# Decay factors carried into the transposing matmuls of q, x copied by ScalarE, and unit 2's norm placed one unit earlier

## The chip, the cores and the metric

The kernel runs on one core of a Trainium2 chip. The engines of that core work side by side, each through its own queue of instructions in order: TensorE (in the profile PE for matmuls, PEld for weight loads), VectorE (DVE), ScalarE (ACT), GpSimd (POOL) and SyncE (SP), which only issues transfers here. A matmul writes to PSUM, of which the kernel has eight banks. The metric is the device time of one execution in microseconds (us); the times given are of several executions, and their median is compared.

## The reference

Two blocks are computed one after the other. The first is a retention layer: attention without softmax, whose scores are weighted by a power of a decay factor for each head.

```python
batch, n_heads, seq, head_dim = (8, 8, 576, 64)
scores = scale * np.matmul(q, k.transpose(0, 1, 3, 2))          # scale = 1/sqrt(64)
gamma = 1.0 - 2.0 ** (-5.0 - np.arange(H))                      # one per head
Dmat = np.where(rel >= 0, gamma[:, None, None] ** rel, 0.0)     # rel = row - column
ret = scores * Dmat
attn_out = np.matmul(ret, v)
```

Its output, with the heads side by side, is x: 8 * 576 = 4608 tokens of 512 numbers. The second block is a feed-forward layer with RMS norm:

```python
rms = np.sqrt(np.mean(x * x, axis=-1, keepdims=True) + 1e-06)
xn = x / rms * rms_g
g = xn @ w_gate                                                 # 512 x 1536
out = (g * (1.0 / (1.0 + np.exp(-g))) * (xn @ w_val)) @ w_out   # 1536 x 512
```

q, k, v and the norm's weights are 32-bit floats; the three large weight matrices come as 64-bit floats and are turned to 32 bits in the kernel.

## The kernel before

**Retention.** There are 32 jobs, one for each batch and pair of heads (`jobs`, line 127). A sequence of 576 is cut into nine chunks of 64 (`L`). Within a chunk the scores are multiplied by v directly (`values`); what earlier chunks contribute is carried in a running sum of k times v (`states` and `sums`) and multiplied by q (`carried`). The decay is split into factors: k's part is put on v by ScalarE (`scale_v`, table `gv`), a constant power of gamma and the causal mask on the scores (`weigh`, line 312), a factor for a whole chunk on the running sum (`gc`), and q's part, gamma to the power of the position in the chunk plus 64, over 8, on the result: `carried` multiplies the two PSUM banks `av` by the table `gq` on VectorE as it writes x (lines 389 to 394). Jobs from 8 on put odd chunks in swapped halves of a bank (`column`) and so also need `gx`, the same table with its halves swapped.

q and k are needed with head elements on the partitions. From job 8 on VectorE transposes them (`prepare`). For the first eight jobs TensorE does it (`turn`, line 216): four 128-token blocks of q for each of two heads as matmuls with the identity `ident` as the moving operand, four blocks of k as transposes, then the last 64 tokens of each as one transpose; ScalarE copies the banks to `qT` and `kT` (lines 235 and 244).

One `slot(j)` (line 397) issues `values` of job j-1, `scores` and `states` of job j, VectorE's `weigh` and `sums` of job j, and `carried` of job j-1. Between `values` and `carried` stands a memset of `tick` on POOL (line 359), which waits for the last matmul of `values`; the first matmul of `carried` waits for it. All these share five PSUM banks (`banks`); three more hold `s`, the scores and states.

**Feed-forward.** x is taken in twelve units of 384 tokens (`U`). Units 0 and 1 go through plain matmuls into the hidden layer (`up_plain`); units from 2 on through a scheme of seven half-size block products instead of eight (`up`). The product with `w_out` uses seven block products for all units (`across`, a generator that hands over after each product). The sums of weight blocks that the scheme needs are made by `combine(m)` on POOL (line 803), twelve 128x512 operations for each of the two weight matrices, and by `combine_out` on VectorE for `w_out`. The hidden layer of unit 1 lies in the part of `w_up[1]` that `combine(1)` writes; the part of `w_up[0]` that `combine(0)` writes holds sums that `across` of units 0 and 1 reads.

**Norm of a unit.** `norm_0`: four squares on ScalarE and three adds on VectorE. `norm_1`: three matmuls with a column of 1/512 into a bank `ms`, an add on VectorE, a power on POOL. `diagonals`: three diagonal matrices on VectorE. `norm_2`: a matmul `rb`, four products that scale x, and, from unit 2 on, four subtractions for the block scheme.

**Order.** The schedule is written out by hand: every engine's queue has its work in program order. `start()` (line 846) loads the tables and the first eight jobs, runs slots 0 to 7 with the turns of the next job between them and with steps of the weights' conversion spread among them (`weights`, `act`), then `up_plain` of units 0 and 1, `across(1)` and `across(0)`. Around these last two stand `combine(1)`, slot 8, unit 2's norm, `combine(0)` and slot 9. Loads are issued by SP, some by ScalarE. The tile framework gives the transfers of both queues eight semaphores in turn, so that one waits for the landing of the one eight before it. From unit 2 on a loop runs `up` and `across` with the other slots between.

Of the kernel before, what the change touches and what calls it, by code (L numbers as in the profile page):

```python
# [10 lines left out]
F32 = mybir.dt.float32  # L11
# [3 lines left out]
P = 128  # L15
# [7 lines left out]
def _decay_tables(H, D):  # L23

    pairs = _gamma(H).reshape(H // 2, 2).T
    rows = np.repeat(pairs, D, axis=0)
    pos = np.arange(L)
    p = np.concatenate([pos, pos])  # L30
    gq = rows[:, :, None] ** (pos + L) / np.sqrt(D)
    t = pairs.T[None] ** -p[:, None, None], rows**L, gq, np.roll(gq, D, axis=0)
    return [np.ascontiguousarray(x).astype(np.float32) for x in t]


# [6 lines left out]
def kernel(  # L42
# [64 lines left out]
    gx = const.tile([P, NHP, L], F32, name="gx")  # L107
    gv = const.tile([P, NHP, 2], F32, name="gv")
    gc = const.tile([P, NHP], F32, name="gc")
    tick = const.tile([1, 1], F32, name="tick")  # L110
    rms_g = const.tile([P, NHP], F32, name="rms_g")
    w_out = const.tile([P, NF, DM], F32, name="w_out")
# [87 lines left out]
    def load_kv(j):  # L200
# [12 lines left out]
            out=t, in_=v[b, 2 * hp : 2 * hp + 2, NFULL * P :].rearrange("e p d -> p e d")  # L213
        )

    def turn(j):

        d = st[j]
        last = bank(f"turn_{j}_t")
        for nm in "qk":  # L220
            ps = bank(f"turn_{j}_{nm}")
            for c in range(NFULL):
                if nm == "k":
                    nc.tensor.transpose(
                        out=ps[:, c * P : c * P + P],
                        in_=d["k"][:, c].rearrange("p e d -> p (e d)"), identity=ident,
                    )
                    continue
                for e in range(2):
                    nc.tensor.matmul(  # L230
                        ps[side(e), c::NFULL], lhsT=d["q"][:, e, c], rhs=ident,
                        start=True, stop=True,
                    )
            t = d[nm + "T"] = att.tile([P, S], F32, tag=nm + "T", name=f"{nm}T_{j}")
            nc.scalar.copy(out=t[:, : NFULL * P], in_=ps)
        for i, nm in enumerate("qk"):
            o = slice(i * TAIL, i * TAIL + TAIL)
            nc.tensor.transpose(
                out=last[:, o], in_=d[nm + "t"].rearrange("p e d -> p (e d)"),
                identity=ident[:TAIL, :TAIL],  # L240
            )
        for i, nm in enumerate("qk"):
            o = slice(i * TAIL, i * TAIL + TAIL)
            nc.scalar.copy(out=d[nm + "T"][:, NFULL * P :], in_=last[:, o])
# [117 lines left out]
    def carried(j):  # L362

        d = st[j]
        b, hp = jobs[j]
        av = d["av"]
        for c in range(1, NC):
            i, odd = divmod(c, 2)
            for e in range(2):
                mm = nc.tensor.matmul(  # L370
                    av[odd][column(j, odd, e), i * L : i * L + L], lhsT=d["sum"][side(e), c - 1],
                    rhs=d["qT"][side(e), c * L : c * L + L],
                    start=False, stop=(c >= NC - 2), skip_group_check=True,
                )
                if c == 1 and e == 0:
                    follow(mm, d["valued"])
        for c0, c1 in ((0, 2 * HU), (2 * HU, S)) if b % 2 == 0 else ((0, HU), (HU, S)):
            u, o = divmod(b * S + c0, U)
            if u not in x_of:
                x_of[u] = xp.tile([P, NHP, U], F32, tag="x", name=f"x_{u}")  # L380
            x = x_of[u][:, hp, o : o + c1 - c0].rearrange("p (c k) -> p c k", k=L)
            for first in (c0 // L, c0 // L + 1):
                i, odd = divmod(first, 2)
                n = -(-(c1 // L - first) // 2)
                moves = [(slice(0, P),) * 2]
                if column(j, odd, 0) != side(0):
                    moves = [(side(e), column(j, odd, e)) for e in range(2)]
                for to, at in moves:
                    g = (gq if to == at else gx)[at, hp].unsqueeze(1)
                    nc.vector.tensor_tensor(  # L390
                        out=x[to, first - c0 // L :: 2],
                        in0=av[odd][at, i * L : (i + n) * L].rearrange("p (c k) -> p c k", k=L),
                        in1=g.to_broadcast([at.stop - at.start, n, L]), op=ALU.mult,
                    )
        st[j] = {}
# [450 lines left out]
    def start():  # L846

        h_of[0] = ffn.tile([P, NF, U], F32, tag="h", name="h_0")
        tables = list(zip((causal, gv, gc, gq, gx), (_causal_table(), *_decay_tables(H, D))))

        def table(i, queue):
            t, values_ = tables[i]
            src = nc.inline_tensor(values_, name=t.tensor.name + "_table")
            queue.dma_start(out=t, in_=src.ap())

        make_identity(nc, ident)
        nc.scalar.activation(out=tick, in_=mhalf[:1], func=AF.Silu)
        nc.vector.memset(ones, 1.0)
        warm = bank("warm")
        for _ in range(6):  # L860
            nc.tensor.matmul(warm[:, :P], lhsT=ones, rhs=ones, start=True, stop=True)
        first_places.update(find_places())
        load_chunks(1)
        for i in (1, 0, 2):
            table(i, nc.scalar)
        weights(3)
        for j in range(2 * NHP):
            load_first(j, {0: range(2), 1: range(2, H), NHP: range(H)}.get(j))
            if j == 1:
                table(3, nc.sync)  # L870
            load_chunks((1, 1, 1, 1, 2, 2, 2, 3)[j], nc.sync)
        table(4, nc.sync)
        nc.sync.dma_start(out=rms_g, in_=moe_rms_g.rearrange("(c p) -> p c", p=P))
        load_chunks(4, nc.sync)
        turn(0)
        scale_v(0)
        act(3)
        squares = []
        for j in range(2 * NHP):
            slot(j)  # L880
            if j + 1 < 2 * NHP:
                turn(j + 1)
            if squares:
                gather(*squares.pop())
            for i in ((1,), (2,), (3,), (4, 5), (6,), (7,), (), ())[j]:
                scale_v(i)
            if j:
                u, c = divmod(j - 1, NHP)
                squares.append((u, c, square(u, c)))
            act(1)  # L890
            if j == 5:
                norm_1(0)
            elif j == 6:
                norm_2(0)
            weights((2, 0, 0, 1, 1, 1, 1, 0)[j])
            if j == 4:
                gather(*squares.pop())
            elif j == 5:
                diagonals(0)
            act(1)  # L900
        gather(*squares.pop())
        load_qk(2 * NHP)
        load_kv(2 * NHP)
        made = combine_out()
        for m, g in [(m, g) for g in range(NG) for m in range(2)]:
            for u in range(2):
                weights_to(4 * g + 2 * m + 1)
                for i, _ in enumerate(up_plain(u, m, g)):
                    if not (u or m or g):
                        if i == 0:  # L910
                            values(2 * NHP - 1)
                            carried(2 * NHP - 1)
                            gather(1, NHP - 1, square(1, NHP - 1))
                        elif i == 1:
                            norm_1(1)
                        elif i == 2:
                            diagonals(1)
                        elif i == 3:
                            norm_2(1)
                    weights(2)  # L920
                    act(1)
                    if u and m and g == NG - 1:
                        weights_to(len(chunks))
                        next(made, None)
                    if i == 1:
                        weights_to(4 * g + 2 * m + 2)
        for _ in made:
            pass
        for blk, t in first_blocks.items():
            keep(blk, t)  # L930
        rest = across(1)
        next(rest)
        following(2 * NHP - 1)
        for _ in rest:
            pass
        rest = across(0)
        next(rest)
        combine(1)
        slot(8, rest=False)
        following(8)  # L940
        for i, _ in enumerate(rest):
            if i in (1, 2, 4):
                (norm_0, norm_1, norm_2)[i // 2](2)
                if i == 2:
                    diagonals(2)
        combine(0)
        slot(9)
        following(9)
# [71 lines left out]
```

## Time and profile before

| | |
|---|---|
| median of 5 executions | 1154.46 us (1152.39 to 1158.57) |
| profiled execution | 1158.57 us, span 1156.8 us, mean granted clock of TensorE 0.993 |
| TensorE busy | 1130.3 us, 98% of the span, 10524 matmuls |
| VectorE busy | 719.2 us (62%) |
| ScalarE busy | 244.0 us (21%) |
| POOL busy | 51.2 us (4%) |
| DMA | 125.42 MB, 108 GB/s on average |
| first matmul of `up_plain` | at 61.6 us |
| `across(1)`, `across(0)` | 191.4 to 218.9 us, 220.0 to 253.5 us |
| first matmul of `up` for unit 2 | at 256.4 us |

All times are counted from the start of the span. In a line of a timeline stand the start, the duration, the engine, the line of the kernel, the operation, what is written and read, the shape and the count; in square brackets the time that the engine stood idle before it and what ended that. In a list of waits stand the one who waited and what it waited for, then the total, the number of times and the longest. "issue" means that the engine waited for nothing that the profile shows. A 32-bit matmul shows as two instructions.

### The profile page before, as it was taken

How to read it: one execution, taken by the hardware profiler on the slowest of the kernel's cores; microseconds unless marked ns; L12 is line 12 of the kernel's file. 1: busy time of each engine (PE TensorE's matmuls, PEld its weight loads, DVE VectorE, ACT ScalarE, POOL GpSimd, SP SyncE). 2: the span in 40 equal slices, each digit the busy share in tenths (PEclk: the TensorE clock that was granted, in tenths of full speed). 3: DMA queues.
4: the chain of work that ended last, by engine and by line, in shares of the span. 5: the costliest groups of instructions: out<-in, count | busy, mean ns of one | idle time of the engine just before them, and what ended most of it. 6: DMA issues, size and time to landing. Idle time of an engine off the chain costs nothing.

```text
span 1156.8 us, 24803 instructions
## 1 busy us (share of the span) xinstructions
PE 1130.3 (98%) x10524; PEld 1056.5 (91%) x10524; DVE 719.2 (62%) x1420; ACT 244.0 (21%) x480; POOL 51.2 (4%) x74
## 2 busy tenths in 40 slices
PE   8899999988999999999999999999999999999998
PEld 7655557988999999999999999999999999999998
DVE  5698867576576575465775776465576576445352
ACT  5545641101211221111220220120220210120210
POOL 0000000480000000000000000000000000000000
PEclk9899999999999999999999999999999999999999
DMA  8765336324553646025335456306436403403304
GB/s 204 202 164 168 109 108 207 64 50 107 132 121 49 167 128 139 39 89 116 96 95 95 106 129 140 116 17 128 104 95 137 130 34 92 128 1 97 122 1 110
DMA packets 292943, 125.42 MB, mean 108 GB/s; under 512 B 270432, under 2 KB 275808, under 8 KB 292832
## 3 DMA queue, kind: packets, MB, share of 16 engines
q1 hardware_dynamic: 282688, 107.66, 37.8%
q10 hardware_dynamic: 10144, 16.16, 4.3%
q8 instruction: 83, 1.36, 0.5%
q14 instruction: 28, 0.23, 0.1%
HBM read 108.83 MB, written 14.94 MB: 107 GB/s over the span
## 4 chain that ended last, share of the span: by engine, by line
PE 87%; DVE 6%; DMA 2%; issue 1%; ACT 1%; SPq 1%; DVEq 0%; POOL 0%; ACTq 0%; POOLq 0%
PE w L507 13%; PE x L507 13%; PE z L507 13%; PE up L564 8%; PE xo L629 7%; PE wo L629 7%; PE zo L629 7%; PE y L507 7%; PE yo L629 4%; PE av L351 2%; PE av L370 2%; PE s L280 1%; PE s L300 1%; DMA w_gate<-in_moe_w_out_dram 1%; DVE sum L329 1%
## 5 line engine op out<-in xcount | busy, mean ns | idle before, releaser
L531 ACT COPY m<-x 128x384 f32<-128x384 f32 x60 | 28.7, 479 | 454.9 <-PE x L507 430.6
L629 PE MATMUL xo<-h,w_out 128*128 128x192 f32 x528 | 90.3, 328 | 0.0
L507 PE MATMUL w<-sums,w_val 128*128 128x192 f32 x480 | 88.6, 328 | 0.6 <-DVE c L514 0.3
L507 PE MATMUL z<-x,w_gate 128*128 128x192 f32 x480 | 87.9, 326 | 1.1 <-DVE u L514 1.1
L507 PE MATMUL x<-x,w_val 128*128 128x192 f32 x480 | 88.7, 328 | 0.0
L507 PE MATMUL x<-x,w_gate 128*128 128x192 f32 x480 | 88.5, 328 | 0.0
L507 PE MATMUL w<-sums,w_gate 128*128 128x192 f32 x480 | 87.8, 326 | 0.0
L507 PE MATMUL z<-x,w_val 128*128 128x192 f32 x480 | 87.8, 326 | 0.0
L629 PEld LDWEIGHTS xo<-h,w_out 128*128 128x128 f32 x528 | 85.9, 190 | 0.6
L629 PE MATMUL wo<-h,w_out 128*128 128x192 f32 x504 | 85.3, 326 | 0.0
L629 PEld LDWEIGHTS wo<-h,w_out 128*128 128x128 f32 x504 | 82.5, 190 | 0.0
L514 DVE TENSOR_TENSOR u<-m,y 128x384 f32<-128x384 f32 x60 | 33.1, 552 | 79.2 <-PE y L507 79.1
L507 PEld LDWEIGHTS w<-sums,w_val 128*128 128x128 f32 x480 | 79.2, 190 | 2.9 <-DVE c L514 2.9
L507 PEld LDWEIGHTS z<-x,w_gate 128*128 128x128 f32 x480 | 79.6, 190 | 1.4 <-DVE u L514 1.4
L507 PEld LDWEIGHTS x<-x,w_val 128*128 128x128 f32 x480 | 79.1, 190 | 0.6
L507 PEld LDWEIGHTS x<-x,w_gate 128*128 128x128 f32 x480 | 79.3, 190 | 0.5
L507 PEld LDWEIGHTS z<-x,w_val 128*128 128x128 f32 x480 | 79.6, 190 | 0.0
L507 PEld LDWEIGHTS w<-sums,w_gate 128*128 128x128 f32 x480 | 79.5, 190 | 0.0
L514 DVE TENSOR_TENSOR h<-u,w 128x384 f32<-128x384 f32 x60 | 33.0, 551 | 69.5 <-PE w L507 69.4
L526 ACT ACTIVATE h<-h 128x384 f32<-128x384 f32 x90 | 47.0, 523 | 89.9 <-DVE h L514 89.9
L564 PE MATMUL up<-x,w_gate 128*128 128x384 f32 x192 | 63.3, 488 | 0.9 <-DVE x L476 0.7
L564 PE MATMUL up<-x,w_val 128*128 128x384 f32 x192 | 62.7, 487 | 0.2 <-ACT w_val L572 0.2
(170 smaller groups left out, 1781.3 us busy)
## 6 DMA issues: line engine op xcount, KB each, us to landing
w_out<-w_blocks SPq DMA_DIRECT2D x70, 768.0 KB, 5.0
out_dram<-o SPq DMA_DIRECT2D x368, 24.0 KB, 1.6
qraw<-in_q_dram SPq DMA_DIRECT2D x96, 72.0 KB, 2.6
kraw<-in_k_dram SPq DMA_DIRECT2D x96, 72.0 KB, 2.7
k<-in_k_dram SPq DMA_DIRECT2D x48, 128.0 KB, 2.8
v<-in_v_dram SPq DMA_DIRECT2D x48, 128.0 KB, 2.9
w_out<-in_moe_w_gate_dram ACTq DMA_DIRECT2D x5, 1024.0 KB, 5.7
w_out<-in_moe_w_out_dram ACTq DMA_DIRECT2D x3, 1024.0 KB, 4.8
```

The costliest lines, as they stand in the source:

```text
L280: nc.tensor.matmul(s[side(odd), e, i * L : i * L + L], lhsT=d["kT"][side(e), c * L : c * L + L], rhs=d["qT"][side(e), c * L : c * L + L], ...
L300: nc.tensor.matmul(o[side(e)], lhsT=d["k"][side(odd), i, e], rhs=d["v"][side(odd), i, e], start=True, stop=True,)
L329: nc.vector.scalar_tensor_tensor(out=t[:, c], in0=t[:, c - 1], scalar=gc[:, hp : hp + 1], in1=part, op0=ALU.mult, op1=ALU.add,)
L351: mm = nc.tensor.matmul(av[odd][column(j, odd, e), i * L : i * L + L], lhsT=d["v"][side(odd), i, e] if c < NC - 1 else d["vt"][:, e], rhs= ...
L370: mm = nc.tensor.matmul(av[odd][column(j, odd, e), i * L : i * L + L], lhsT=d["sum"][side(e), c - 1], rhs=d["qT"][side(e), c * L : c * L + L],
L507: nc.tensor.matmul(ps[:, i * HU : i * HU + HU], lhsT=w_up[m][:, 2 * blk + c, cut], rhs=t_of[u][blk][:, c], start=(start and i == c == 0), ...
L514: nc.vector.tensor_tensor(out=o, in0=a, in1=pairs_of(ps), op=ALU.add)
L526: nc.scalar.activation(out=o, in_=c, func=AF.Silu)
L531: nc.scalar.copy(out=s1, in_=pairs_of(x_))
L564: nc.tensor.matmul(ps[:, :U], lhsT=w_up[m][:, 4 * half + c, i * P : i * P + P], rhs=x_of[u][:, c], start=(c == 0), stop=(c == NHP - 1),)
L629: nc.tensor.matmul(ps[:, i * HU : i * HU + HU], lhsT=a[:, c, i * P : i * P + P], rhs=rhs[:, c], start=(start and i == c == 0), stop=False, ...
```

## The change

There are three parts.

1. A new table `turned` holds q's decay factor for every token place of `turn` and every head: for each of 128 partitions and 8 heads five numbers, four for the 128-token blocks and one for the tail. `make_factors(j, engine)` spreads it onto the diagonal of the identity, which gives per head four 128x128 blocks and a 64x64 one; they lie in parts of `w_up` that the conversion of the weights fills later. The factors of a pair of heads serve job j and job j+4. VectorE makes those of pair 0, POOL those of pairs 1 to 3. `turn` uses them as the moving operand in place of the identity, and turns q's tail by two matmuls where one transpose was.
2. `carried` of the first eight jobs therefore only copies, and ScalarE does it. `gq` is first used by job 8, and its load goes from behind job 1's loads to behind job 7's. `turned` is the first load on ScalarE's queue.
3. `norm_0` of unit 2 is issued after the second product of `across(1)`, `norm_1` and `diagonals` after the fourth; `norm_2` in `across(0)` after the third product, where it was after the fifth.

```diff
@@ _decay_tables
     t = pairs.T[None] ** -p[:, None, None], rows**L, gq, np.roll(gq, D, axis=0)
+    at = np.stack([(4 * np.arange(P) + i) % L for i in range(4)] + [np.arange(P) % L], axis=1)
+    t += (_gamma(H)[None, :, None] ** (at[:, None, :] + L) / np.sqrt(D),)
@@
+    turned = const.tile([P, H, NFULL + 1], F32, name="turned")
@@
+    def factors(j, e):
+        h = 2 * jobs[j][1] + e
+        main = w_up[0][:, h, 2 * P : 6 * P].rearrange("p (i t) -> p i t", t=P)
+        return main, w_up[1][:TAIL, h, 4 * P : 4 * P + TAIL]
+
+    def make_factors(j, engine):
+        for e in range(2):
+            main, tail = factors(j, e)
+            g = turned[:, 2 * jobs[j][1] + e]
+            engine.tensor_tensor(
+                out=main, in0=ident.unsqueeze(1).to_broadcast([P, NFULL, P]),
+                in1=g[:, :NFULL].unsqueeze(2).to_broadcast([P, NFULL, P]), op=ALU.mult,
+            )
+            engine.tensor_tensor(
+                out=tail, in0=ident[:TAIL, :TAIL],
+                in1=g[:TAIL, NFULL:].to_broadcast([TAIL, TAIL]), op=ALU.mult,
+            )
@@ turn
-                        ps[side(e), c::NFULL], lhsT=d["q"][:, e, c], rhs=ident,
+                        ps[side(e), c::NFULL], lhsT=d["q"][:, e, c], rhs=factors(j, e)[0][:, c],
...
-        for i, nm in enumerate("qk"):
-            o = slice(i * TAIL, i * TAIL + TAIL)
-            nc.tensor.transpose(
-                out=last[:, o], in_=d[nm + "t"].rearrange("p e d -> p (e d)"),
-                identity=ident[:TAIL, :TAIL],
-            )
+        for e in range(2):
+            nc.tensor.matmul(
+                last[side(e), :TAIL], lhsT=d["qt"][:, e], rhs=factors(j, e)[1],
+                start=True, stop=True,
+            )
+        nc.tensor.transpose(
+            out=last[:, TAIL : 2 * TAIL], in_=d["kt"].rearrange("p e d -> p (e d)"),
+            identity=ident[:TAIL, :TAIL],
+        )
@@ carried
                 for to, at in moves:
+                    if j < 2 * NHP:
+                        nc.scalar.copy(
+                            out=x[to, first - c0 // L :: 2],
+                            in_=av[odd][at, i * L : (i + n) * L].rearrange("p (c k) -> p c k", k=L),
+                        )
+                        continue
@@ start
+        table(5, nc.scalar)
         load_chunks(1)
         for i in (1, 0, 2):
             table(i, nc.scalar)
+        for j in range(NHP):
+            make_factors(j, nc.gpsimd if j else nc.vector)
         weights(3)
         for j in range(2 * NHP):
             load_first(j, {0: range(2), 1: range(2, H), NHP: range(H)}.get(j))
-            if j == 1:
-                table(3, nc.sync)
             load_chunks((1, 1, 1, 1, 2, 2, 2, 3)[j], nc.sync)
+        table(3, nc.sync)
         table(4, nc.sync)
@@ start, across(1)
-        for _ in rest:
-            pass
+        for i, _ in enumerate(rest):
+            if i == 1:
+                norm_0(2)
+            elif i == 3:
+                norm_1(2)
+                diagonals(2)
@@ start, across(0)
         for i, _ in enumerate(rest):
-            if i in (1, 2, 4):
-                (norm_0, norm_1, norm_2)[i // 2](2)
-                if i == 2:
-                    diagonals(2)
+            if i == 2:
+                norm_2(2)
         combine(0)
```

More of the change, by code (lines that the diff above doesn't have):

```diff
@@ L848, in start @@
         h_of[0] = ffn.tile([P, NF, U], F32, tag="h", name="h_0")
-        tables = list(zip((causal, gv, gc, gq, gx), (_causal_table(), *_decay_tables(H, D))))
+        tables = list(zip((causal, gv, gc, gq, gx, turned), (_causal_table(), *_decay_tables(H, D))))
         def table(i, queue):
```

## The prediction

> **What bounds the kernel now.** First the page: TensorE is 98% busy, so time is lost only where it stands still. Then TensorE's list of waits names those places (columns: total us, times, longest).
>
> ```profile
> PE 1130.3 (98%) x10524; PEld 1056.5 (91%) x10524; DVE 719.2 (62%) x1420; ACT 244.0 (21%) x480; POOL 51.2 (4%) x74
> ...
> PE av L370 <- issue: 7.2, 4, 2.9
> PE ms L450 <- DVE sq L438: 2.7, 1, 2.7
> PE z L507 <- DVE u L514: 1.1, 1, 1.1
> PE av L370 <- POOL tick L359: 1.0, 3, 0.4
> ```
>
> The change aims at the second line and at VectorE in the first 70 us. Next the timeline around unit 2's norm, TensorE and then POOL. To see: `ms` stands 2.72 us for VectorE's sums, yet at 255.75 TensorE waits again, for a POOL memset that sits behind both runs of `combine`.
>
> ```profile
> 227.95 4.06 PE L629 MATMUL wo<-h,w_gate 128*128 128x192 f32 x24
> 234.73 0.80 PE L450 MATMUL ms<-mean_w,sq 128*128 128x1 f32 x6 [2.72 <-DVE sq L438]
> 235.39 5.83 PE L629 MATMUL yo<-h,w_gate 128*128 128x192 f32 x24
> ...
> 255.75 0.69 PE L370 MATMUL av<-qT,sum 64*64 64x64 f32 x32 [0.41 <-POOL tick L359]
> ...
> 264.20 1.57 PE L507 MATMUL z<-x,w_gate 128*128 128x192 f32 x8 [1.06 <-DVE u L514]
> ...
> 217.36 19.69 POOL L811 TENSOR_TENSOR w_val<-w_val 128x512 f32<-128x512 f32 x12 [145.37 <-DMA out_dram<-o]
> 237.01 0.86 POOL L456 TENSOR_TENSOR r<-r,mhalf 128x3 f32<-128x3 f32 x1
> 237.84 17.82 POOL L811 TENSOR_TENSOR w_gate<-w_gate 128x512 f32<-128x512 f32 x12
> 255.61 0.09 POOL L359 MEMSET tick<- 1x1 f32 x1
> ```
>
> Last, one early slot in the timeline, and the table by stage (busy us per engine, granted clock, DMA share, GB/s). To see: `values` starts when ScalarE has copied kT out of a bank, while VectorE holds the two `av` banks to 27.5; and after a stall of 2.88 us TensorE ran at half clock for 10 us.
>
> ```profile
> 25.46 0.59 ACT L235 COPY qT<-turn_q 128x512 f32<-128x512 f32 x1 [2.57 <-PE turn_q L230]
> 26.04 0.59 ACT L235 COPY kT<-turn_k 128x512 f32<-128x512 f32 x1
> 26.58 0.94 DVE L390 TENSOR_TENSOR x<-av,gq 128x192 f32<-128x192 f32 x4
> 26.68 0.85 PE L351 MATMUL av<-ret,first_t 64*64 64x64 f32 x30 [0.24 <-ACT kT L235]
> ...
> 35.50:38.40 2.90, 0.02 (x2) 0.01 (x1) 2.58 (x10) 1.75 (x6) 0.00 (x0) 0.91 1.12 247
> 38.40:48.70 10.30, 9.97 (x192) 8.94 (x194) 4.29 (x13) 6.36 (x13) 0.09 (x1) 0.53 0.91 259
> ```
>
> The profiled execution took 1158.57 us (span 1156.8, 1.8 around it), the slowest of five; their median is 1154.46. I sum against 1158.57 and carry the difference over to the median. 0.3% (3.5 us) is about what this kernel's measurement can tell from no change.
>
> **The change part by part.**
>
> *Table and factors.* `turned` (20 KB) goes first on ScalarE's queue; an issue there takes 0.40 to 0.44 us, so chunk 0 and three small tables go that much later. The 32 KB `causal` landed in 2.5 us, so `turned` is there at about 3.4. Job 0's factors are two 128x512 products and two small ones on VectorE: by 0.55 us for 128x384 and 1.32 for 128x1152, 0.68 each, 1.8 in all. Beside POOL's own factors it may be slower: the three `sq` adds beside `combine` took 4.69 us, 1.55 each instead of 0.55. `turn_q` needs the third product: at 4.9 or, contended, 8.1. Its 2 us then end at 6.9 or 10.1, and TensorE waits for k until 8.11 anyway: 0 to +2.0, I take +0.5, nearer the short end because POOL's pauses let VectorE in. Behind them on VectorE stands chunk 0's first weight step (6.67); it may slip by the 3.18 us that VectorE idles before 12.41. POOL's factors are six products of 1.27 to 1.59 and six small ones (0.29 at most, the row of `ident`): 9.4 to 11.3 us, done by 14.7; job 1's third is needed at 12.3, job 2's at 18.7, job 3's at 24.3: covered. Without `gq` SP is 1.65 us earlier from 12.75 and 128 KB lighter (0.6 us at 223 GB/s): counted below. `gx`, `gq` are now first read at 257.
>
> *Turn.* The main matmuls are as many as before. The q tail becomes two fp32 matmuls of two passes for one transpose: +3 matmuls and +3 loads per job, about 0.1 us while TensorE waits for kT (0.24 to 0.38): 0; without that cover 0.8 in all.
>
> *x on ScalarE.* Four copies per job. Rows: 128x512 0.59, 128x384 0.48, 128x64 0.22, so about 0.33, 0.33, 0.28, 0.22, overlapping to 0.8 to 1.0 us. ScalarE idled 2.57 before qT, and TensorE's `turn_q` takes 1.05 after `carried`: hidden, or +0.2 in seven slots if not. VectorE loses 0.94 a job. The banks come free at 25.3, so `values` need not wait for kT; next late is ScalarE's scaling of v (done 27.88, before `states` at 28.0). So 0.2 of the 0.55 is left, three slots: -0.6 (0 to -1.5). Jobs 4 and 5 hang on loads that land at 31.4 and 37.1; the missing `gq` pays there what the queue loses. From 53.7 to 65.0 the chain of waits is VectorE's; 0.94 of it goes, but the up product ends at 64.4: -0.6; `values` at 58.08, held by banks, -0.4; later sums -0.4: -1.4 (-0.5 to -2.5). Front: -1.5 (+3 to -4).
>
> *Norm of unit 2.* Squares and sums now fall at 196 to 200, where VectorE is idle and POOL too: 3 x 0.55. `ms` comes after unit 1's `yo`: 0.7 us of TensorE that moves, but 0.7 us ahead of `wo`, whose reading of h lets `combine(1)` start at 217.36. The power and the diagonals run at 210 to 212, no one waits. In unit 0 the 2.72 and the slow `yo` (1.8 us of half clock) go: 4.5 us. Against it, `norm_2` now sits before `yo`'s sums on VectorE: 2.2 us plus four subtractions beside POOL (5.3), so u4 is done at 241.9 and `zo` waits 0.8. TensorE reaches `carried(8)` at about 251.2. There it waits: the memset is behind 24 `combine` products. POOL: start +0.7, less the power (-0.8), less the slowing by sums and diagonals (three POOL products of 1.58, 1.45, 1.46 instead of 1.27: -0.7): 254.8 instead of 255.6. So of 4.5 us 0.8 is left (0 to 1.6), and 3.6 become a wait. VectorE's backlog at 255 to 263 is gone, so most of the wait of 1.06 goes too: -1.9 in all.
>
> *The clock.* A gap of 2.72 us gave 3.4 us of half clock, one of 2.88 gave 10.2, one of 2.50 (at 278.3) none. 3.6 us at 251 is longer than all: I take one stretch of 3.4 us, +1.7. Part: -0.2 (from -2.9 to +3.2, with three stretches). The Trainium skill (TensorE: Matmul & The Clock Gate, "HAM oscillation") speaks against this change: idle gaps over some 3.4 us lower the clock. By that page the half clock comes for certain, with the same sum, though it would not have come after the 2.72 us of this trace, where it did.
>
> *Instruction blocks.* The waits by "issue" are not work. Counting TensorE's instructions ahead of the stalls at 30.3, 35.5, 60.5, 278.3 and 301.8 gives 1216, 1473, 2496, 5057, 5568: each 192 or 193 above a multiple of 256; and one of the two instruction queues moved 83 packets for TensorE's 21,200 instructions, one per 256. The 2.50 at 278.3 came where a boundary fell 2 matmuls into a slot of 140, so that the next fell inside the same 2.9 us; 6 into it cost 1.26, 9 nothing. The change adds 48 instructions ahead, 24 matmuls: these two stalls (3.8 us) go, but the slots at 632, 653, 821 and 841 then have boundaries 6, 9, 4 and 8 into them: by the same rows 1.3 + 0.2 + 1.8 + 0.5 = 3.8. Six more slots get a boundary 1 to 9 matmuls before them; one 1 before the slot at 253.5 cost nothing, one 2 before that at 58.1 cost 0.54: 0, or up to 1 each. Sum 0 (-3.8 to +6). The Trainium skill (Runtime: NRT & Kernel Launch, "Instruction fetch mechanics") calls crossing a block mostly hidden; by that page the term is 0 with no spread, while this trace shows 3.8 us.
>
> Sum: -1.5 - 0.2 + 0 = -1.7: 1156.9 for this execution, **1152.7** against the median.
>
> **The rivals.**
> *Blocks fall well:* the counts are off by a few waits and the later slots stay clean. Then -1.7 - 3.8: 1149.0. For it: boundaries 9 or more into a slot cost nothing. Against: 4 and 6 are near the 2 and 6 that cost.
> *Blocks fall badly (slower):* the place is the twelve slots from 362 to 865 with a boundary between 9 before and 12 into them; at 0.54 (the row at 60.5) for the six before and 1.26 (that at 301.8) for five of the six inside they cost 9.5, less the 3.8 that go: 1152.7 + 5.7 = 1158.4. For it: a boundary 15 before the slot at 33.3 cost 2.88, though under a saturated DMA. Against: 9 to 23 into a slot cost nothing in seven slots. It decides when a fetch starts only with the slot, as at 278.3, and not some 3 us ahead as at 250.2.
> *The clock stays low:* the gap before `carried(8)` halves it for three stretches, as at 38.4: 5.1 us instead of 1.7: 1156.1. Against: the matmuls after it are dense, as after 234.7, where one stretch was all.
> *ScalarE becomes the front's bound:* its x copies stand behind the scaling of v(5), which waits for a load until 37.1, and a weight step of 1.15; +0.9 in three slots instead of -1.5: 1156.9.
> *POOL's wait does not come* (its start is not moved): the 4.5 us stay: 1149.5. The memset behind `combine` in program order speaks against it.
>
> **How the numbers follow.** Forecast 0.40; blocks well 0.20, badly 0.18; clock 0.10; POOL 0.07; ScalarE 0.05. Range 1146 to 1160: below it the good blocks with the front 3 us better, above it the bad blocks with one term more; 2 in 10 are left out. Faster by over 0.3% (below 1151.0): most of the good blocks and of POOL (0.23) and a quarter of the forecast: 0.34; slower (above 1157.9): 0.13 of the bad blocks and 0.10 of clock, front and forecast: 0.23; between: 0.43. The forecast alone: 1150 to 1156.
>
> **What would show it.** `ms` of unit 2 near 207 with no wait; a wait of about 3.6 us of `av` for `tick` near 251 and POOL's memset within 1 us of before; half clock after it; no `x` product on VectorE before 255 and `values` ahead of the kT copy's end; issue stalls near 632 and 821 and none at 278. Wrong if TensorE passes 255 without a wait, or if the front moves by over 3 us.

## The result and the profile after

The changed kernel takes 1158.31 us, the median of 33 executions (1154.99 to 1163.05), against 1154.74 us of 59 executions of the kernel before. The ratio is 1.0034 with a 95% interval of 1.0026 to 1.0043: the change costs about 3.9 us, where 1.7 us less had been forecast (1152.7).

The profiled execution of after took 1157.38 us (span 1155.6), less than the profiled execution of before (1158.57). The two profiles laid side by side therefore do not show the loss at all: the one of before was the longest of its first five executions, 3.8 us over the median. A second profile of each was taken among the experiments below; that of before took 1154.78 us, about the median, and is the one to compare with. That of after took 1161.66 us, 3.4 over its median, so of after the first one (0.9 under it) is the nearer.

The page of after, first busy times, then TensorE's list of waits (total us, times, longest):

```profile
PE 1129.0 (98%) x10548; PEld 1056.1 (91%) x10548; DVE 716.7 (62%) x1392; ACT 250.0 (22%) x512; POOL 61.6 (5%) x86
...
PE av L397 <- issue: 6.3, 4, 3.2
PE av L397 <- POOL tick L386: 4.1, 4, 3.1
PE turn_t L261 <- DVE w_val L235: 1.8, 1, 1.8
PE turn_q L254 <- DVE w_gate L231: 1.6, 2, 0.9
PE x L540 <- issue: 1.4, 1, 1.4
PE s L307 <- issue: 1.4, 1, 1.4
...
PE zo L662 <- DVE u4o L671: 0.8, 1, 0.8
```

The wait of `ms` (2.7) is gone, that of `z` (1.1) too. In their place stand the wait for `tick`, new waits of the turn for the factors, and the waits by "issue", which are 9.1 us now (6.3 + 1.4 + 1.4). The second profile of before has 6.5 of these, 5.3 of them in `av`:

```profile
PE av L370 <- issue: 5.3, 4, 2.9
PE ms L450 <- DVE sq L438: 2.7, 1, 2.7
PE turn_k L224 <- DMA first_k<-in_k_dram: 1.9, 1, 1.9
PE av L370 <- POOL tick L359: 1.4, 3, 0.8
```

Three places of after's timeline. The start (VectorE, then TensorE): VectorE's second small factor, a 64x64 product, takes 5.30 us beside POOL's factors, and the tail of job 0 waits for it, so the first scores start at 12.14 (10.01 before).

```profile
6.32 5.30 DVE L235 TENSOR_TENSOR w_val<-ident,turned 64x64 f32<-64x64 f32 x1
...
11.68 0.33 PE L261 MATMUL turn_t<-w_val 64*64 64x64 f32 x2 [1.81 <-DVE w_val L235]
...
12.14 0.83 PE L307 MATMUL s<-qT,kT 64*64 64x64 f32 x40
```

The norm: the wait for POOL's memset is there, and the matmuls after it run at half clock (8 in 2.07 and 2.68 us, later 8 in 1.47; the granted clock is 0.50 from 255.8 to 259.2).

```profile
254.28 0.69 PE L397 MATMUL av<-qT,sum 64*64 64x64 f32 x32 [3.13 <-POOL tick L386]
254.91 2.07 PE L540 MATMUL x<-x,w_gate 128*128 128x192 f32 x8
256.77 2.68 PE L540 MATMUL y<-sums,w_gate 128*128 128x192 f32 x8
259.29 1.47 PE L540 MATMUL z<-x,w_gate 128*128 128x192 f32 x8
```

And a late slot: 24 of 32 matmuls of `carried` run, then TensorE stands 1.63 us for nothing that the profile shows.

```profile
839.00 0.56 PE L397 MATMUL av<-qT,sum 64*64 64x64 f32 x23
841.20 0.34 PE L397 MATMUL av<-qT,sum 64*64 64x64 f32 x8 [1.63 <-issue]
841.47 1.57 PE L540 MATMUL x<-x,w_gate 128*128 128x192 f32 x8
```

There are four of these from 640 us on: 0.71, 0.71, 1.63 and 1.45, 4.50 in all. In the second profile of after they are 1.65, 0.96, 1.86 and 1.47, 5.94. The question for the experiments was which part of the change brings the loss, and what sets the length of these stalls.

### The profile page after: what moved, and what is told of

It reads as the page before. It is cut to its first block, busy times and chain, and to the rows that moved or that the text cites. A ratio compares the mean times of both kernels' runs of the same rounds, so it can differ in the third digit from the quotient of the medians.

```text
span 1155.6 us, 24873 instructions
## 1 busy us (share of the span) xinstructions
PE 1129.0 (98%) x10548; PEld 1056.1 (91%) x10548; DVE 716.7 (62%) x1392; ACT 250.0 (22%) x512; POOL 61.6 (5%) x86
## 4 chain that ended last, share of the span: by engine, by line
PE 94%; DVE 2%; POOL 2%; ACT 1%; issue 1%; DMA 0%; DVEq 0%; POOLq 0%
PE x L540 14%; PE w L540 14%; PE z L540 13%; PE up L597 10%; PE xo L662 8%; PE wo L662 8%; PE zo L662 8%; PE y L540 7%; PE yo L662 4%; PE av L397 2%; PE av L378 2%; POOL w_gate L844 1%; PE s L307 1%; PE s L327 1%; PE rb L507 1%
```

## The experiments

### One part at a time

The third part alone on the kernel before:

```diff
-        for _ in rest:
-            pass
+        for i, _ in enumerate(rest):
+            if i == 1:
+                norm_0(2)
+            elif i == 3:
+                norm_1(2)
+                diagonals(2)
...
-            if i in (1, 2, 4):
-                (norm_0, norm_1, norm_2)[i // 2](2)
-                if i == 2:
-                    diagonals(2)
+            if i == 2:
+                norm_2(2)
```

> Part 3 alone: unit 2's norm at its new places, q, x and the tables as before. If the wait of carried(8) for the memset on POOL and the half clock behind it are what makes the change slower, this is 1 to 3 us slower than before, and its profile shows the wait of about 3 us near 251 and a stretch of half clock after it. If the loss is in the first 70 us or in where the instruction blocks end, this is 0 to 1.5 us faster than before (the gain of 0.9 us from up(unit 2) on that the two profiles show), with the stalls at 278 and 301 still there.

Measured: 1152.98 us, ratio 0.9979 (0.9965 to 0.9993). The same edit taken back out of the changed kernel:

> Parts 1 and 2 without part 3. If the loss is in the front or in the blocks, this is as much slower than before as the whole change, by 3 to 5 us. If it is the norm's new place, this is within 1 us of before.

Measured: 1161.51 us, ratio 1.0048 (1.0033 to 1.0064). The norm is a gain: 2.4 us alone; on top of the other parts about 1.6, though there the two intervals overlap. The other parts lose 5.5 us (3.8 to 7.4).

Only the tail of q, turned by two matmuls with the plain identity where one transpose was; this adds the change's 48 TensorE instructions to the kernel before and nothing else:

```diff
-        for i, nm in enumerate("qk"):
-            o = slice(i * TAIL, i * TAIL + TAIL)
-            nc.tensor.transpose(
-                out=last[:, o], in_=d[nm + "t"].rearrange("p e d -> p (e d)"),
-                identity=ident[:TAIL, :TAIL],
+        for e in range(2):
+            nc.tensor.matmul(
+                last[side(e), :TAIL], lhsT=d["qt"][:, e], rhs=ident[:TAIL, :TAIL],
+                start=True, stop=True,
             )
+        nc.tensor.transpose(
+            out=last[:, TAIL : 2 * TAIL], in_=d["kt"].rearrange("p e d -> p (e d)"),
+            identity=ident[:TAIL, :TAIL],
+        )
```

> The kernel before with one edit: q's tail of the first eight jobs turned by two matmuls with the identity, so that 48 instructions of TensorE are added ahead of the later slots and nothing else changes. If the place of the instruction blocks decides, the stalls at 278 and 301 (3.8 us) go, new ones come near 640, 660, 840 and 925 (4 us together in the profile after), and the time moves by the difference of the two and by what the blocks do in the first 70 us: up to 4 us either way. If the blocks do not matter for the median, it is within 0.5 us of before.

Measured: 1159.90 us, ratio 1.0036 (1.0024 to 1.0048). 48 small instructions, 0.8 us of TensorE's time by the prediction's estimate, cost 4.2 us: as much as the whole change. Its late stalls stand where those of after do (650.7, 672.7, 841.4, 926.5; 0.99 + 1.26 + 1.51 + 1.10 = 4.86; the profile puts the last down to VectorE's `sum`, but it stands at the end of a block of 256 and, as the others, 1.4 us behind the landing of an instruction packet, of which below).

The start: all factors on VectorE, so that POOL does not run beside it.

```diff
-            make_factors(j, nc.gpsimd if j else nc.vector)
+            make_factors(j, nc.vector)
```

> The whole change, but VectorE makes all factors and POOL none. In the profile after, VectorE's second 64x64 product took 5.3 us beside POOL's factors and the first scores started at 12.1 instead of 10.0. If that is the loss, the small product takes 0.2 us, the scores start by 10.5 and the kernel is about 2 us faster than the whole change (1 to 2 us slower than before instead of 3.6). If the front is set by loads or by block fetches, the time stays at 3 to 4 us over before.

Measured: 1159.58 us, ratio 1.0029 (1.0015 to 1.0042). The first scores come at 10.32 again, and yet `up_plain` starts at 61.34 (after: 60.61 and, in its second profile, 63.55): repairing the start by 1.8 us moves nothing that stands clear of the noise.

The x copies by ScalarE alone, on the kernel before (q's factor is left out of these eight jobs):

```diff
                 for to, at in moves:
+                    if j < 2 * NHP:
+                        nc.scalar.copy(
+                            out=x[to, first - c0 // L :: 2],
+                            in_=av[odd][at, i * L : (i + n) * L].rearrange("p (c k) -> p c k", k=L),
+                        )
+                        continue
```

> The kernel before, with x of the first eight jobs only copied, by ScalarE; the multiplication by gq is left out of those jobs, and nothing stands in for it, so this is part 2 alone, without the tables, the factors, or the tail's 48 instructions. My prediction priced it at -0.6 for the early slots and -1.4 for the late ones: 1153. Theory 'ScalarE becomes the front's bound': +0.9, 1156. Theory 'the front stands for instruction blocks behind saturated loads, so work taken off VectorE is only a longer stall': no change, 1155.

Measured: 1154.73 us beside 1156.31 of before, ratio 0.9993 (0.9980 to 1.0005). Worth 0.8 us or nothing; not the 2.0 that I had given it, and not a loss.

### Second profiles of both kernels

> The kernel before once more, for a second profile. The first profiled execution took 1158.57 us, 3.8 over the median. If its stalls at 278.3 and 301.8 (3.76 in all) are typical, the excess lies in the front: its first matmul of up_plain at 61.60, where three kernels with the same front have 58.6 to 59.3; then it is near 59 here and the two stalls are here again. If the excess is the two stalls, they are shorter here and the first matmul of up_plain is near 61.

Measured: 1154.78 us. Both halves of the excess show: the front is quicker (first matmul of `up_plain` at 57.88, not 61.60) and the two stalls of 2.50 and 1.26 are 0.92 and 0.71. Some of it goes back: a stall of 0.53 at 570.7, and 1.6 us more from the first product of `across(1)` to the `z` product at 262, with longer half clock.

> The changed kernel once more, for a second profile. If the front is where it loses against the typical execution of before, the first matmul of up_plain is again at 60.6 to 61.8 with a start of scores near 12; if only the late stalls are the loss, at 59. The late stalls near 650, 671, 840 and 924 come again, 0.7 to 2.2 us each, as long as they hang on which packets of the weight load the instruction fetch finds ahead of it.

Measured: 1161.66 us, `up_plain` at 63.55, first scores at 12.45, late stalls 5.94. Stalls at one place thus differ from run to run by a factor of two, though the instructions are the same.

### Why TensorE stands

The trace also records each DMA packet. TensorE's instructions come in packets of 16 KB on a queue of their own, one per 256 instructions (83 packets for 21271 instructions in after); where one block of 256 ends and the next begins, call it a crossing. All the late stalls stand at a crossing, most of them at the second of two that lie close together in and behind a slot. For such pairs of after and before:

```
          first      second     last 6 KB packet   instruction packet   TensorE   stall
          crossing   crossing   that ends there                         goes on
after     626.85     628.72     none running       625.82 to 626.74     -         0
after     647.82     649.78     647.98 to 648.25   648.25 to 649.19     650.49    0.71
after     669.52     671.49     669.54 to 669.78   669.78 to 670.81     672.20    0.71
after     837.66     839.57     838.60 to 838.83   838.83 to 839.78     841.20    1.63
after     860.20     862.08     none running       858.97 to 860.22     -         0
after     921.48     924.47     923.28 to 923.51   923.51 to 924.51     925.91    1.45
before    276.38     278.30     278.29 to 278.53   278.53 to 279.48     280.80    2.50
```

The 6 KB packets are the loads of weight blocks for `w_out`'s products, line 642 (two blocks of 768 KB, some 5 us). In the stalled rows the instruction packet starts 2 to 3 ns after one of those packets ended (in the last of after, within 3 ns); before's row is the plainest, where that was the last 6 KB packet still on its way. With up to 17 of them under way such a match can be chance; in 14 of the 43 late stalls (over 0.4 us, behind 250 us, all seventeen profiles) at most three others were, and there the packet starts 2 or 3 ns behind the end of one every time. After the instruction packet has landed TensorE needs 1.2 to 1.6 us more, at all 90 stalls of over 0.4 us at a crossing in the seventeen profiles. So the packet is the one that the second crossing needs: at 626.85 and 860.20 TensorE passed the first without a stand, 0.1 us after that packet landed or before. Where no load runs, the packet starts 1.0 to 1.2 us ahead of the first crossing, 2.9 to 3.1 ahead of the second, and from its start to TensorE's going on it is 2.2 to 2.4 us in the stalled rows. The delay by a load therefore costs only what exceeds the rest. Ordinary products use up a block in some 21 us (128 matmuls, 8 of them in 1.30 us), a slot in about 2 us, so it shows only where two crossings lie within 2 or 3 us. If so, moving the loads must take the stalls away without touching an instruction of TensorE:

```diff
-                if i in (1, 3):
-                    fetch()
+                for _ in range((2 if i in (1, 3) else 0) if u % 3 == 1 else 4 if i == 0 else 0):
                     fetch()
```

> The changed kernel, with the loads of the weight blocks for the products with w_out taken earlier: in units with slots at the first products all four loads are issued at the first up product, instead of two at the second and two at the fourth. TensorE's instructions and their blocks stay where they are. In the profile of the changed kernel each late stall has the same form: the packet of the instruction queue starts only when 6 KB packets of those loads have drained (838.83 after a chain that ends at 838.83; stall 1.63 us at 839.57), while slots without such a load fetch about 1.1 us ahead of the crossing and stand nowhere. Theory 'the fetch waits behind a weight load': the stalls near 650, 671, 840 and 924 (0.71 + 0.71 + 1.63 + 1.45 = 4.5 us) go, 1153 to 1154.5. Theory 'two blocks in 2.1 us are too many wherever the loads are': they stay, 1158. Theory 'the loss lies in the first 70 us': 1158 as well.

Measured: 1155.25 us, ratio 1.0001 (0.9988 to 1.0013), 3.8 us less than after by the ratios. TensorE's waits between 600 and 960 us, first of after:

```profile
PE av L397 <- issue: 3.0, 3, 1.6
PE x L540 <- issue: 1.4, 1, 1.4
PE av L397 <- POOL tick L386: 0.3, 1, 0.3
```

then of after with the earlier loads:

```profile
PE av L397 <- issue: 1.7, 1, 1.7
PE av L397 <- POOL tick L386: 0.3, 1, 0.3
```

All four are gone, with TensorE's instructions unchanged; one new stall of 1.69 stands at 820, where the moved loads now lie beside a slot that had been free. The same edit on the kernel before and on the third part alone:

> The kernel before with the same earlier loads. Theory 'the fetch waits behind a weight load': its two late stalls (2.50 at 278.3 and 1.26 at 301.8 in the profiled execution, which was the slowest of five) go: 1151 if they are as long in the median execution, 1153.5 if the median has only a third of them. Theory 'two blocks in 2.1 us are too many wherever the loads are': no change, 1155.

> The kernel before with only the third part of the change (unit 2's norm among unit 1's out products) and the earlier loads. Theory 'the fetch waits behind a weight load': the stalls at 295.9 (1.10) and 569.2 (1.18) of the run with the third part alone go: 1150.5 to 1152, below both kernels. Theory 'two blocks in 2.1 us': as that run, 1153.

Measured: 1155.85 (ratio 0.9997, 0.9983 to 1.0010) and 1153.78 (0.9987, 0.9972 to 1.0002). No gain in either. In both the stall at 302 (296 with the third part) went. But the slot at 275 has one of 1.78 and 1.80, and in both the instruction packet starts within 4 ns of the end of a packet of the moved loads; the kernel before had stalled there already (2.50 and 0.92), the third part alone had not. The expectation was wrong in leaving that out: where a kernel has few stalls, moving the loads exchanges them.

The other way round: the loads stay, the 48 instructions go. q's tail is scaled in SBUF and turned by one transpose as before (scaled by POOL; by VectorE for job 0), and `make_factors` makes no factors for the tail:

```diff
+        heads = slice(2 * jobs[j][1], 2 * jobs[j][1] + 2)
+        (nc.gpsimd if j else nc.vector).tensor_tensor(
+            out=d["qt"], in0=d["qt"],
+            in1=turned[:TAIL, heads, NFULL:].to_broadcast([TAIL, 2, D]), op=ALU.mult,
+        )
...
-        for e in range(2):
-            nc.tensor.matmul(
-                last[side(e), :TAIL], lhsT=d["qt"][:, e], rhs=factors(j, e)[1],
-                start=True, stop=True,
+        for i, nm in enumerate("qk"):
+            o = slice(i * TAIL, i * TAIL + TAIL)
+            nc.tensor.transpose(
+                out=last[:, o], in_=d[nm + "t"].rearrange("p e d -> p (e d)"),
+                identity=ident[:TAIL, :TAIL],
```

> The changed kernel, but q's last 64 tokens are scaled by their factors in SBUF (64x128 on POOL, for job 0 on VectorE) and turned by one transpose as before, so TensorE has the kernel before's 10524 matmuls again; the 48 instructions of the tail are gone, the rest of the change stays. Theory 'the 48 instructions shift the blocks': the stalls near 650, 671, 840 and 924 go, those near 296 and perhaps 569 come as in the run with the third part alone (4.5 less, 1.1 to 2.3 more): 1155 to 1156.5. Theory 'the front's new work (factors, x on ScalarE) is what costs': 1158.

Measured: 1155.29 us, ratio 1.0000 (0.9988 to 1.0013). Between 600 and 960 no stall of a slot is left; those at 297 (1.26) and 570 (0.97) are back. Its start is the worst of all (3.91 us for VectorE's scaling of job 0, which stands behind a weight step), and still `up_plain` begins at 59.65. So the front, too, seems to lose through the 48 instructions more than through the start. With the scaling on ScalarE, where job 0 waits 0.55 us only:

```diff
+        for e in range(2):
+            nc.scalar.activation(
+                out=d["qt"][:, e], in_=d["qt"][:, e], func=AF.Copy,
+                scale=turned[:TAIL, 2 * jobs[j][1] + e, NFULL:],
+            )
```

> The changed kernel, but q's last 64 tokens are scaled in SBUF by ScalarE (two 64x64 activations per job) and turned by one transpose as before: TensorE has 10524 matmuls again, and job 0 waits neither for VectorE's small product nor, as in the run that did this on POOL and VectorE, 3.9 us for a VectorE that stands in the weights' conversion. Theory 'the front lost through the blocks that the 48 instructions moved': the first matmul of up_plain comes at 58 to 59, where before it came at 57.9 in the median execution and in the changed kernel at 60.6 to 63.6; with the norm's gain 1153 to 1154. Theory 'the front lost through the late start of job 0': up_plain near 58 too, but then the run that only repaired the start (all factors on VectorE), which began up_plain at 61.3, should have shown it. Theory 'factors and x copies cost by themselves': 60.5 or later, 1155.5 or more.

Measured: 1153.48 us, ratio 0.9977 (0.9962 to 0.9992), `up_plain` at 59.09. This is the changed kernel in all but the tail, 6.6 us faster by the ratios, and as fast as the third part alone (0.9979).

Over all profiles: `up_plain` starts at 61.95 on average in the six with the 48 instructions (60.61 to 63.55) and at 59.03 in the eleven without (56.22 to 61.60), 2.9 us apart. Only part of that shows as stalls: ahead of `up_plain` the waits by "issue" are 5.1 us on average in the six and 3.9 in the eleven, the other waits 5.6 and 6.7, and TensorE is busy for 50.9 and 48.1 us. That the 48 instructions cost the front some 3 us is shown; that they do it at the crossings is shown for 1.2 us at most. The late stalls are 4.50 to 6.65, 5.7 on average, in the five that have the instructions and the loads where they were, and 1.05 to 3.76, 2.3 on average, in the eight with the loads in place and without the instructions: 3.4 us apart.

### The wait behind combine

The third part alone, with the memset of `tick` for job 8 on VectorE:

```diff
-        d["valued"] = nc.gpsimd.memset(tick, 0.0)
+        d["valued"] = (nc.vector if j == 2 * NHP else nc.gpsimd).memset(tick, 0.0)
```

> The kernel before with only the third part of the change, and one memset more moved: the write to tick between values and carried of job 8 goes from POOL, where it stands behind the 24 products of combine, to VectorE, which is idle there. In the run with the third part alone TensorE stood 3.13 us at 249.1 for that memset and then ran at half clock for one stretch of 3.4 us. Theory 'the norm's gain is held back by the memset': the wait goes and the half clock with it, 3.1 + 1.7 = 4.8 us, 1148 to 1149.5; some of it may come back where the first up products of unit 2 wait for VectorE. Theory 'the up products of unit 2 have to wait for combine in any case': no change, 1153.

Measured: 1151.23 us beside 1156.31, ratio 0.9960 (0.9945 to 0.9974). TensorE's timeline of this run at that place:

```profile
248.99 0.68 PE L370 MATMUL av<-qT,sum 64*64 64x64 f32 x31
249.60 1.57 PE L507 MATMUL x<-x,w_gate 128*128 128x192 f32 x8
251.00 1.46 PE L507 MATMUL y<-sums,w_gate 128*128 128x192 f32 x8
...
257.00 1.54 PE L507 MATMUL z<-x,w_gate 128*128 128x192 f32 x8 [0.63 <-DVE u L514]
```

No wait, no half clock; 0.63 comes back at `z`, as had been allowed for. Against the run without it the products from `z` to the slot at 269 come 4.0 us earlier. The times show 2.2 of that (0.9979 to 0.9960, and the two intervals overlap): the slot at 271 now meets a weight load and stalls 1.74, and behind that stall TensorE runs at half clock for 3.4 us (granted 0.51; 8 matmuls in 1.88 and 2.77 us). Two variants went after the rest. Tail scaled by ScalarE and this memset:

> The same, with the memset of tick of job 8 on VectorE, so that it does not stand behind POOL's products of combine. If the two gains add up, 2.2 to 3.3 us below the run without it: 1150 to 1151.5, as fast as the third part with that memset alone (1151.2) or a little faster, since VectorE has less to do in the front. If the front's parts 1 and 2 are worth nothing or less even without the 48 instructions, it is slower than that run: 1152 or more.

Measured: 1153.19 us, ratio 0.9973 (0.9961 to 0.9986): the memset adds nothing there. Its profile has a stall of 3.44 at 30.9 and one of 2.60 at 272.7, with half clock behind it, in place of 1.91 and a wait of 3.15 in the run without the memset. And the third part with the memset, and the loads of units 2, 5, 8 and 11 between the slots:

```diff
-                if i in (1, 3):
+                if i in ((2, 4) if u % 3 == 2 else (1, 3)):
```

> The third part with the memset of tick for job 8 on VectorE, and in the units with slots at the second, fourth and sixth up product (2, 5, 8, 11) the weight blocks are loaded two at the third and two at the fifth product instead of at the second and fourth, so that they no longer run while a slot does. In the run without this the fetch stood behind a 6 KB packet once, 1.74 us at 271.1; in the kernel with tail_act's front and the same memset the same place cost 2.60. Theory 'the fetch waits behind a weight load': that stall goes and none comes at 293 or 569; 1149.5 against 1151.2, and the best of all kernels. Theory 'two blocks in 2.1 us are too many in that slot wherever the loads are': the stall at 271 stays, 1151.

Measured: 1148.48 us beside 1153.61, ratio 0.9957 (0.9940 to 0.9974). The stall at 271 is gone as expected; two others, 1.19 at 289 and 0.75 at 311, came under the moved loads, which I had not expected, so the ratio is that of the run without this edit. Either is 4.6 to 5.0 us faster than before by its ratio, and 8.5 to 8.9 faster than the changed kernel.

## Why the prediction was wrong

Forecast 1152.7, measured 1158.3. The time is that of the rival "blocks fall badly" (1158.4), but the account under it is another.

**Instruction blocks, the step that failed.** "These two stalls (3.8 us) go, but the slots at 632, 653, 821 and 841 then have boundaries ... Sum 0." The two old stalls went, and boundaries fell into those four slots, but about four matmuls earlier than counted (2, 5, 0 and 4 into them instead of 6, 9, 4 and 8), so that two more slots had them (8 and 7). Mis-sized were both sides. The 3.8 that go are those of a long execution: in the median one they are 1.6 (0.92 + 0.71). And the new ones are 4.5 to 5.9 instead of 3.8, at other slots than the rule said: the slots with boundaries 0, 2 and 7 matmuls in cost nothing, those with 4, 5 and 8 cost 1.63 to 1.86, 0.71 to 1.65 and 0.71 to 0.96, and one came in the product after a slot, at 924. I had read a rule of position from three rows (2, 6 and 9). Position decides only how close the next boundary is; whether it costs is decided by a weight load that runs when the packet is due. By the averages of the profiles the term was +3.4 and not 0. The rival's condition, a fetch that starts only with the slot, came close: it starts when the load lets it.

**Front -1.5: +2.9.** I counted blocks for the late slots only, although the longest stall of the trace, 2.88, was in the front. The 48 instructions cost there as well (tail alone: `up_plain` at 62.58; without them, in the changed kernel, at 59.09 and 59.65). "0 without that cover 0.8 in all" was the price of their work alone. How they cost the rest stays open: 1.2 us of it show as longer stalls, and which boundary costs what was not taken apart. The DMA is busy throughout there (share 0.86 to 1.06 from 10 to 50 us in the first profile of before), and at the same instruction, the 1217th, the stalls range from 0.4 to 3.8.

**Its parts.** *Start +0.5:* 2.1, the contended end, and by POOL as described. It decides nothing: with it repaired the front is no quicker. *x on ScalarE:* hidden, as said; the four copies take 0.83 us, and `values` starts at 23.14, ahead of the end of kT's copy at 23.37. The gain of 2.0 did not arrive: 0.8 at most by the run with it alone, and with the whole front but the tail none over the third part alone. *POOL's factors:* covered.

**Norm of unit 2, -0.2.** The wait of 2.72 went, `zo` waits 0.75 (0.8 forecast), `tick` 3.13 (3.6), one stretch of half clock follows, the wait of `z` is gone. All came, and the sum is still better than forecast: -2.4 (-4.0 to -0.8) by the run with it alone, some -0.9 by the traces (from 160 to 268 us the eight profiles with the third part and the memset on POOL take 0.9 less, on average, than the six without the part). One reason shows in the trace: the half clock after the wait of 2.72 cost before 1.8 us in the first profile but more in the second, where `yo` takes 7.12 instead of 5.83 us:

```profile
230.76 1.18 PE L450 MATMUL ms<-mean_w,sq 128*128 128x1 f32 x6 [2.72 <-DVE sq L438]
231.79 7.12 PE L629 MATMUL yo<-h,w_gate 128*128 128x192 f32 x24
```

The rest, between the two measures, I can't place. In both profiles of before half clock follows the gap of 2.72 us. The Trainium skill (TensorE: Matmul & The Clock Gate, "HAM oscillation") names only gaps of over some 3.4 us as the ones to avoid; here the shorter one had the same effect.

**Sum.** Front +2.9, late slots +3.4, norm -0.9 to -2.4: +3.9 to +5.4, measured +3.9. These are averages over several kernels. The two profiles nearest the medians, the first of after and the second of before, give +3.4 up to the first product of `across(1)` (190.87 against 187.47), -2.1 from there to the `z` product at 263, and +1.3 behind it: +2.6. The rivals of the clock, of ScalarE and of the absent POOL wait did not come about. (The last is 1148.5 by its own terms, -1.5 - 4.5, and not 1149.5; nothing hangs on it.) The Trainium skill (Runtime: NRT & Kernel Launch, "Instruction fetch mechanics") calls a crossing mostly hidden; the term by it was 0. The runs show 3.4 us at the late crossings.

## What to carry to other kernels

Where TensorE is busy 98%, count its instructions: a dense stretch that uses up a block of 256 in 2 us can stand if a large load is under way when the next block is to come. So 48 instructions more far ahead cost 4 us here, and issuing the loads earlier (at 630 us instead of 643 and 664, for one unit) gave 3.8 back; in the two kernels with few such stalls the same move gave nothing. Before pricing what a change removes, look whether the profiled execution is a typical one: a stall that differs from run to run is worth its median. And a memset that only passes a signal is better off on an engine that has nothing long in its queue: moved, it took a wait of 3.1 us out of the trace, although the time showed 2.2 of it in one kernel and nothing sure in another, where other stalls grew.

## What was unexpected

- A gap of the same length does not give the same clock. After the 2.7 us wait for `sq` TensorE ran at a granted clock of 1.00 in one run (the tail alone), at half for some 3.4 us in the first profile of before, and for 6.8 in the second. Inside a slot a stall of 1.74 us (at 271, the third part with the memset on VectorE) was followed by half clock and one of 2.50 (at 278, the first profile of before) was not. What decides it these runs do not show. The table by stage, busy us per engine, granted clock, DMA share and GB/s, first of the tail alone, where the clock, third from the row's end, is 1.00 in both rows:

```profile
232.30:235.00 2.70, 0.02 (x1) 0.00 (x0) 2.50 (x2) 0.00 (x0) 2.54 (x3) 1.00 0.88 177
235.00:239.00 4.00, 3.95 (x26) 3.98 (x27) 0.93 (x2) 1.49 (x4) 3.92 (x4) 1.00 0.25 56
```

then of the second profile of before, 0.50 and 0.64:

```profile
228.00:231.00 3.00, 0.28 (x4) 0.27 (x3) 2.51 (x2) 0.00 (x0) 2.84 (x3) 1.00 0.92 183
231.00:235.00 4.00, 4.00 (x15) 4.00 (x16) 1.22 (x2) 1.49 (x4) 3.92 (x4) 0.50 0.20 41
235.00:239.00 4.00, 4.00 (x18) 4.00 (x17) 1.68 (x4) 0.00 (x0) 3.33 (x4) 0.64 0.00 0
```

- A 64x64 product on VectorE stood 5.30 us while POOL made its factors, through four of POOL's 128x512 products and the small ones between them; with POOL idle the first scores start 1.8 us earlier.
